# Attention and two MLPs on one core: one tile per PSUM bank in place of tiles of two banks, and another order of the first block

## The chip, the core and the metric

The kernel runs on one core of a Trainium2 chip. A core has a matrix engine (TensorE, PE in the profile), a vector engine (DVE), a scalar engine (ACT), GpSimd (POOL) and SyncE (SP), which here issues all the transfers. Each engine works through its own list of instructions in order; engines wait for each other at semaphores. Matrix results go to PSUM, which has eight banks; a bank holds 512 fp32 values in each of 128 partitions. The metric is the device time of one execution in microseconds, lower is better.

## The reference

The reference is a chunked attention, then an MLP that takes the maximum of three projections, then a second MLP with a piecewise square.

```python
for c in range(nc):                       # 24 chunks of 32 queries; B=4, H=8, S=768, D=64
    k_full = concat([mem_k, k[l_start:r_end]])     # 8 memory keys, 16 left, 32 own, 8 right
    scores = scale * q_c @ k_full.T
    a = exp(scores - max(scores)); a = a / (sum(a) + 1e-9)
    out[c] = a @ v_full
x = out.reshape(3072, 512)
h = maximum(maximum(x @ w1, x @ w2), x @ w3)       # 512 -> 768
x = h @ w_out                                      # 768 -> 512
h = x @ w_in                                       # 512 -> 2048
g = where(h >= 1, h, where(h <= -1, 0, (h + 1)**2 / 4))
out = g @ w_out2                                   # 2048 -> 512
```

## The kernel before

The 3072 tokens are six blocks of 512, and each block is four attention units of 128 tokens (24 units, `u`). Every product of the MLPs is done with operands split into a high and a low part, so one product is three matmuls (`mm3`, L510: high by high, high by low, low by high).

A unit runs: transposes of K and Q (`st_k` L262, `st_q` L293), scores (`st_s`, 32 small matmuls into two banks, one for even heads `e=0` and one for odd heads `e=1`), the row maximum and its subtraction (`st_m` L381, on DVE), exp (`st_e`), row sums and division (`st_n`), the transpose of the weights (`st_a`), the product with V (`st_o`, again two banks), its copy to SBUF (`cp_o` L438), and the transpose and split that give the MLP its input (`st_x`, `cp_x`, `cp_xl` L456).

PSUM is held in tiles of two banks. The scores and the outputs of a unit take a whole such tile (`ps_pair`, L212); the other steps take its two halves in turn (`ps_bank`, L207). In block 0 there are four pairs; from the step `l0` on, one pair is left to attention (L744), two banks (`ps_mm`) belong to the first product of either MLP, and four banks, as two tiles of two (`ps_acc`), hold the sums of the second product.

Those sums are filled slot by slot: `slot_l2` (L551) adds one of the K1 = 6 parts of the first MLP, `slot_l4` (L600) one of the K2 = 16 parts of the second, to the four banks `acc[0..3]`, three matmuls each. In the last slot of a block, each bank is copied out right after its three matmuls: in `slot_l2` by ACT (L565), in `slot_l4` by ACT for `t` 0 and 2 (L617) and by DVE for 1 and 3 (L615).

All engines' lists are written by hand. Block 0 follows the table `PLAN` (L40), a list of step names: `f` loads a raw weight, `wa wh wg ws wp` turn it into the high and low parts (`convert_w`, `hi_w`, `rest_w`, `sub_w`, `add_w`, L125 to L168), `l3` is one product of 12 matmuls, `lt` its maximum, `m0` one `slot_l2`, `d` four small matmuls with nothing but the identity, `lk lq lv lm` loads, and the others the steps of a unit. Further tables say which engine takes a step (`ON_DVE`, `NORM_ON_POOL`, `ABS_ON_ACT` and so on). From block 1 on the order comes from loops (L749): a slot of 12 matmuls, then one step of a later block's attention. In the second MLP the slots alternate, `slot_l4(n)` then `slot_l3(n+3)` (L758).

Of the kernel before, what the change touches and what calls it, by code (L numbers as in the profile page):

```python
# [39 lines left out]
PLAN = """  # L40
lq0 f0 lmem0 wa0 d0 wg0 tq0 lk1 d7 lk0 mem0 f1 wh0 d4 tk1 ws0 ck1 wa1 tk0 wp0 ck0 lq1 f2 lk2 ek0 tq1
ek1 lq2 kw0 cq1 cq0 s0 tk2 lq3 wh1 lk3 ck2 ws1 tq2 tk3 lk4 wg1 wa2 ek2 cq2 mx0 wh2 ex0 d5 wp1 kw1
lm0 tq3 f3 lq4 tk4 wg2 n0 ck3 f4 s1 ek3 a0 kw2 ws2 lk5 ck4 cq3 mx1 lv0 ek4 s2 wp2 wa3 f5 d1 mx2 tq4
tk5 ex1 wg3 wh3 ws3 wa4 kw3 mv0 lv1 ex2 s3 ck5 wp3 n1 wh4 wg4 ca0 lq5 lv2 mv2 cq4 a1 n2 ek5 mv1 o0
co0 ws4 a2 wa5 x0 kw4 ca1 wh5 mx3 f6 o1 tq5 wg5 s4 co1 wp4 ca2 lk6 ex3 ws5 wa6 f7 kw5 lk7 wg6 tk6
lv3 wp5 n3 wa7 mx4 lk8 wh6 o2 ck6 cq5 x1 ws6 wp6 cx0 wh7 cx1 a3 dx0 ex4 f8 wg7 co2 ca3 dx1 n4 ws7
wa8 tk7 ck7 o3 x2 lq6 cx2 s5 f9 co3 wp7 wh8 x3 a4 wg8 mx5 dx2 cx3 dx3 wa9 lv4 tk8 ws8 tq6 ca4 l3 wg9
f10 o4 l0 ex5 wh9 n5 ws9 wp8 wp9 ek7 ek6 wa10 co4 lt3 wg10 wh10 l1 lt0 lt1 l2 f11 wa11 ws10 lv5 lt2
wg11 lm1 cq6 x4 f12 wp10 lh2 wh11 cx4 l4 f13 l5 wa12 wg12 ws11 wp11 lt4 lt5 wh12 a5 dx4 l6 wa13 d6
f14 lk9 wg13 wh13 ws12 ws13 lq7 l7 wp12 lt6 wa14 ca5 lh5 kw6 o5 co5 f15 s6 mx6 wh14 lt7 lv6 wg14 ex6  # L50
l9 wp13 ws14 wp14 lt9 f16 wa15 x5 ck8 n6 tq7 cq7 l10 cx5 wh15 dx5 lt10 wg15 lk10 l8 a6 wa16 ws15 lt8
ek8 ca6 f17 kw7 l11 s7 lt11 wg16 wp15 wa17 m0 l12 wh16 mv6 f18 lm2 mx7 ws16 wg17 wp16 lh8 f19 ex7
wa18 wh17 ws17 m1 wh18 o6 wp17 ws18 l13 co6 d2 wg18 wp18 wa19 lt12 tk9 lq8 wh19 x6 wg19 f20 cx6 ck9
dx6 lt13 m2 n7 f21 lv7 wa20 wh20 wg20 ek9 ws19 wp19 ws20 d3 l14 a7 lt14 tq8 cq8 l15 ca7 wa21 f22
wp20 wa22 o7 lh11 wh21 f23 co7 wh22 lh14 ws22 wg22 l16 kw8 wp22 x7 wg21 ws21 cx7 wp21 m3 lt15 l17
dx7 lt16 s8 lq9 mx8 lk11 wa23 wh23 ws23 wg23 lt17 m4 ex8 wp23 lq10 lv8 lh17
# [12 lines left out]


@with_exitstack
def attention_then_two_mlps(ctx, tc, q, k, v, mem_k, mem_v, w1, w2, w3, w_mid, w_in, w_out, out):
# [132 lines left out]
    pairs, turn = [ps_t.tile([P, 2, TB], F32, name="pt")], [0]

    def ps_bank():  # L207
        i = turn[0] = turn[0] % (2 * len(pairs))
        turn[0] += 1
        return pairs[i // 2][:, i % 2] if not isinstance(pairs[i // 2], list) else pairs[i // 2][i % 2]  # L210

    def ps_pair():  # L212
        i = (turn[0] + 1) // 2 % len(pairs)
        while isinstance(pairs[i], list):
            i = (i + 1) % len(pairs)
        turn[0] = 2 * i + 2
        return pairs[i]

# [629 lines left out]
```

## Time and profile before

| what | value |
|---|---|
| median of 3 runs (lowest to highest) | 1109.12 us (1107.56 to 1109.77) |
| the profiled execution: its time, its span | 1109.17 us, 1107.4 us |
| PE busy | 1038.5 us, 94% of the span |
| weight load (PEld) busy | 833.9 us, 75% |
| DVE busy | 544.8 us, 49% |
| ACT busy | 346.2 us, 31% |
| POOL busy | 243.3 us, 22% |
| mean granted TensorE clock | 0.975 of full |

The span counts from the first to the last instruction of the profiled execution. A row of the trace gives an instruction's start, its duration, engine and source line, what it writes and reads, and in square brackets the idle time of its engine just before and the instruction that ended it. Matmuls overlap in the array: a matmul of 512 columns is shown as 0.39 us long, and the next one starts 0.23 us after it. So the idle time before a matmul is counted from the end of that 0.39, and the distance from one start to the next says more.

### The profile page before, as it was taken

To read this page: it belongs to the slowest core of one execution; us is meant where nothing else is said; L and a number is where in the kernel's file an instruction comes from. 1 tells how busy PE (TensorE), PEld (TensorE's weight loads), DVE (VectorE), ACT (ScalarE), POOL (GpSimd) and SP (SyncE) were. 2 spreads that over 40 slices of the span, in tenths; PEclk is the share of its full clock that TensorE was granted. 3 is DMA by queue.
4 is the path that set the end of the run, shared out by engine and by line. 5 is a ranking of instruction groups with operands and counts; after the bars stand their busy time and mean duration, and the time that the engine had idled before them with its cause. 6 is when DMAs were issued, how large, how long until landed. Compare 5 with 4: busy or idle time off the path is not lost.

```text
span 1107.4 us, 18192 instructions
## 1 busy us (share of the span) xinstructions
PE 1038.5 (94%) x7426; PEld 833.9 (75%) x7426; DVE 544.8 (49%) x896; ACT 346.2 (31%) x609; POOL 243.3 (22%) x193
## 2 busy tenths in 40 slices
PE   6488999999999999999899989989999998998998
PEld 4376768878877778878688868868877886886886
DVE  7999947678777777534454222222222222222221
ACT  4754543342233232243433222212222222222221
POOL 2423221011011011112123213312322321331221
PEclk9689999999999999999899989989999999999999
DMA  9744536556556563243321010010001001001001
GB/s 220 175 130 121 157 80 162 120 139 163 132 139 167 113 171 92 91 133 124 105 66 29 1 49 20 10 47 10 20 1 48 29 1 48 20 1 39 0 1 39
DMA packets 163940, 88.89 MB, mean 80 GB/s; under 512 B 126736, under 2 KB 144144, under 8 KB 163856
## 3 DMA queue, kind: packets, MB, share of 16 engines
q1 hardware_dynamic: 163856, 87.72, 29.6%
q8 instruction: 58, 0.95, 0.4%
q14 instruction: 26, 0.21, 0.1%
HBM read 67.24 MB, written 20.45 MB: 79 GB/s over the span
## 4 chain that ended last, share of the span: by engine, by line
PE 81%; DVE 11%; ACT 3%; issue 2%; SPq 1%; DMA 0%; POOL 0%; ACTq 0%; DVEq 0%; POOLq 0%
PE l L511 15%; PE l L512 15%; PE l L513 15%; PE o L609 8%; PE o L611 8%; PE o L610 8%; PE y L511 3%; PE y L512 2%; PE y L513 2%; PE pt L435 1%; PE pt L371 1%; DVE c_a L136 1%; DVE c_a L138 1%; SPq L345 1%; ACT y L565 1%
## 5 line engine op out<-in xcount | busy, mean ns | idle before, releaser
L596 DVE SCALAR_TENSOR_TENSOR u<-u 128x512 f32<-128x512 f32 x96 | 66.6, 694 | 359.5 <-ACT u L595 359.5
L523 POOL TENSOR_TENSOR hl_b<-u,hh_b 128x512 fp32r<-128x512 f32 x96 | 123.8, 1290 | 409.3 <-ACT hh_b L521 197.9
L511 PE MATMUL l<-xh,hi_a 128*128 128x512 f32 x432 | 175.3, 406 | 4.5 <-DVE xl L458 2.8
L609 PE MATMUL o<-hi_d,hh_b 128*128 128x512 f32 x384 | 152.9, 398 | 17.9 <-ACT ob L617 17.9
L512 PE MATMUL l<-xl,hi_a 128*128 128x512 f32 x432 | 169.4, 392 | 0.0
L513 PE MATMUL l<-xh,lo_a 128*128 128x512 f32 x432 | 169.4, 392 | 0.0
L511 PE MATMUL l<-yh,hi_c 128*128 128x512 f32 x384 | 152.6, 397 | 0.0
L512 PE MATMUL l<-yl,hi_c 128*128 128x512 f32 x384 | 152.4, 397 | 0.0
L513 PE MATMUL l<-yh,lo_c 128*128 128x512 f32 x384 | 152.0, 396 | 0.0
L611 PE MATMUL o<-hi_d,hl_b 128*128 128x512 f32 x384 | 151.4, 394 | 0.0
L610 PE MATMUL o<-lo_d,hh_b 128*128 128x512 f32 x384 | 151.4, 394 | 0.0
L595 ACT ACTIVATE u<-l 128x512 f32<-128x512 f32 x96 | 57.3, 597 | 250.5 <-PE l L513 209.8
L523 POOL TENSOR_TENSOR hl_a<-t,hh_a 128x512 fp32r<-128x512 f32 x33 | 45.0, 1364 | 333.6 <-ACT hh_a L521 333.6
L521 ACT CAST hh_b<-u 128x512 fp32r<-128x512 f32 x96 | 59.6, 620 | 146.2 <-DVE u L597 146.2
L609 PEld LDWEIGHTS o<-hi_d,hh_b 128*128 128x128 f32 x384 | 72.7, 189 | 38.9 <-ACT ob L617 23.6
L511 PEld LDWEIGHTS l<-xh,hi_a 128*128 128x128 f32 x432 | 81.3, 188 | 22.4 <-DVE xl L458 3.0
L513 PEld LDWEIGHTS l<-xh,lo_a 128*128 128x128 f32 x432 | 81.4, 188 | 18.3 <-DVE lo_a L168 0.4
L512 PEld LDWEIGHTS l<-xl,hi_a 128*128 128x128 f32 x432 | 81.6, 189 | 15.2
L511 PEld LDWEIGHTS l<-yh,hi_c 128*128 128x128 f32 x384 | 73.6, 192 | 16.3
L512 PEld LDWEIGHTS l<-yl,hi_c 128*128 128x128 f32 x384 | 73.6, 192 | 16.4
L513 PEld LDWEIGHTS l<-yh,lo_c 128*128 128x128 f32 x384 | 73.5, 191 | 16.4
L611 PEld LDWEIGHTS o<-hi_d,hl_b 128*128 128x128 f32 x384 | 73.0, 190 | 16.0
(167 smaller groups left out, 1334.4 us busy)
## 6 DMA issues: line engine op xcount, KB each, us to landing
st_a<-in_moe_w_dram SPq DMA_DIRECT2D x18, 512.0 KB
vw<-in_v_dram SPq DMA_DIRECT2D x160, 56.0 KB
st_c<-in_moe_w_in_dram SPq DMA_DIRECT2D x16, 512.0 KB
st_d<-in_moe_w_out_dram SPq DMA_DIRECT2D x16, 512.0 KB
yd<-y SPq DMA_DIRECT2D x24, 256.0 KB
yr<-yd SPq DMA_DIRECT2D x24, 256.0 KB
out_dram<-ob SPq DMA_DIRECT2D x24, 256.0 KB
wd<-c_c SPq DMA_DIRECT2D x16, 256.0 KB
```

The lines of the kernel that those rows point to most:

```text
L136: V.tensor_scalar(out=c, in0=c, scalar1=3, scalar2=0x3FFFFFFF, op0=ALU.logical_shift_left, op1=ALU.bitwise_and)
L138: V.scalar_tensor_tensor(out=c, in0=up, scalar=0xC0000000, in1=c, op0=ALU.bitwise_and, op1=ALU.bitwise_or)
L511: nc.tensor.matmul(ps, whi, xhi, start=first, stop=False)
L512: nc.tensor.matmul(ps, whi, xlo, start=False, stop=False)
L513: nc.tensor.matmul(ps, wlo, xhi, start=False, stop=last)
L521: nc.scalar.copy(out=hi, in_=h)
L523: e.tensor_tensor(out=lo, in0=h, in1=hi.bitcast(F32), op=ALU.subtract)
L595: nc.scalar.activation(out=a, in_=ps, func=AF.Relu, bias=0.5, scale=0.5)
L596: nc.vector.scalar_tensor_tensor(out=a, in0=a, scalar=1.0, in1=a, op0=ALU.min, op1=ALU.mult)
L609: nc.tensor.matmul(acc[t], hi[:, c], whi, start=first, stop=False)
L610: nc.tensor.matmul(acc[t], hi[:, c], wlo, start=False, stop=False)
L611: nc.tensor.matmul(acc[t], lo[:, c], whi, start=False, stop=last)
```

## The change

Every PSUM tile becomes one bank. `ps_tile` takes the next pool in the list `psum_turn`: eight turns over the pools `t`, `mm` and `acc0` to `acc3` up to `l0`, after that only the two banks of `ps_t`. The scores and outputs of a unit are two tiles, one for each parity `e`; the maximum and the subtraction (`st_m`) and the copy of the outputs (`cp_o`) become one instruction for each parity, of half the size. The sums of the second products are four tiles with tags of their own, `acc0` to `acc3`. `PLAN` has the same 388 step names in another order, and the tables that choose engines differ.

```diff
-lq0 f0 lmem0 wa0 d0 wg0 tq0 lk1 d7 lk0 mem0 f1 wh0 d4 tk1 ws0 ck1 wa1 tk0 wp0 ck0 lq1 f2 lk2 ek0 tq1
...
+f0 d7 d6 f1 lk0 tk0 lq0 wa0 lm0 lk1 ck0 wa1 lmem0 tq0 wg1 mv0 mv1 lq1 ek0 wh0 lq2 ws0 tk1 ck1 ek1
...
-ca4 co1 cq1 cq4 ek2 ek5 mem0
+ck1 co4 co5 ek0 ek1 ek6 kw0 mem0 mv0
...
-NORM_ON_POOL = "n1 n2 n3 n6 n8".split()
-ABS_ON_ACT = "a1.1 a0.2 a1.2 b.1 a2.2 a0.3 b.2 a0.4 a1.4 b.3 a2.4 a0.5 a1.5 b.4 a2.5 b.5".split()
-LOW_ON_POOL = "a1.0 a2.1 a1.2 a1.3 b.5".split()
-SUB_ON_DVE = "a0.0 a2.0 a1.1 a0.2 a1.2 b.1 a0.3 a1.3 a2.3 a0.4 b.3 a2.4 a1.5 b.4 a2.5".split()
-ADD_ON_DVE = "a1.0 a0.1 b.0 b.1 a0.3 a1.3 a1.4 b.3 a2.4 b.4 a2.5".split()
-SPLIT_ON_DVE = "a0_3 a0_1 a0_2".split()
-SUM_ON_ACT = [5]
+NORM_ON_POOL = "n4 n6".split()
+ABS_ON_ACT = "a0.0 a1.1 b.1 a2.2 a1.3 b.2 a2.3 a0.4 a1.4 a2.4 a0.5 a1.5 b.4 a2.5 b.5".split()
+LOW_ON_POOL = "a1.0 b.0 a1.2 b.2 b.4 b.5".split()
+SUB_ON_DVE = "a1.0 b.1 a0.3 b.2 a2.3 a0.4 b.3 a0.5 a1.5 b.4 a2.5".split()
+ADD_ON_DVE = "a0.0 a1.0 a1.1 a2.1 a0.2 b.1 a1.3 a2.3 b.3 a2.4 a1.5 b.4 a2.5".split()
+SPLIT_ON_DVE = "a0_0 a0_1 a0_2".split()
+SUM_ON_ACT = [7]
...
-    ps_t = ctx.enter_context(tc.tile_pool(name="ps_t", bufs=1, space=PSUM))
+    ps_t = ctx.enter_context(tc.tile_pool(name="ps_t", bufs=2, space=PSUM))
...
+    psum_turn = []
+
+    def ps_tile(name):
+        pool, tag = psum_turn[0]
+        psum_turn.append(psum_turn.pop(0))
+        return pool.tile([P, TB], F32, tag=tag, name=name)
...
-        s = ps_pair()
+        s = [ps_tile(f"s{u}_{e}") for e in range(2)]
...
-        nc.vector.tensor_reduce(out=m, in_=sg, axis=AX.X, op=ALU.max)
+        for e in range(2):
+            nc.vector.tensor_reduce(out=m[:, e], in_=sg[e], axis=AX.X, op=ALU.max)
...
-            nc.vector.tensor_tensor(
-                out=p.rearrange("p h e j -> p e h j"), in0=sg, in1=m.to_broadcast([P, 2, HP, NK]), op=ALU.subtract)
+            for e in range(2):
+                nc.vector.tensor_tensor(
+                    out=p[:, :, e], in0=sg[e], in1=m[:, e].to_broadcast([P, HP, NK]), op=ALU.subtract)
...
-        copy("co", u)(out=xs[u].rearrange("p (h e d) -> p e h d", h=HP, e=2), in_=pp.pop(("o", u)))
+        for e, o in enumerate(pp.pop(("o", u))):
+            copy("co", u)(
+                out=xs[u].rearrange("p (h e d) -> p e h d", h=HP, e=2)[:, e],
+                in_=o[:, 0:HP * D].rearrange("p (h d) -> p h d", h=HP))
...
-            if f == 0 and d % 2 == 0:
-                t = ps_acc.tile([P, 2, TB], F32, tag="acc", name=f"y{j}_{d}", bufs=2)
-                acc[d], acc[d + 1] = t[:, 0], t[:, 1]
+            if f == 0:
+                acc[d] = ps_acc.tile([P, TB], F32, tag=f"acc{d}", name=f"y{j}_{d}")
...
-            if first and t % 2 == 0:
-                o2 = ps_acc.tile([P, 2, DM], F32, tag="acc", name=f"o{i}_{t}", bufs=2)
-                acc[t], acc[t + 1] = o2[:, 0], o2[:, 1]
+            if first:
+                acc[t] = ps_acc.tile([P, DM], F32, tag=f"acc{t}", name=f"o{i}_{t}")
...
+        psum_turn += [(ps_t, "t"), (ps_mm, "mm"), (ps_acc, "acc0"), (ps_acc, "acc1"),
+                      (ps_t, "t"), (ps_mm, "mm"), (ps_acc, "acc2"), (ps_acc, "acc3")]
```

Three places show what this does to the engines' lists. The first is on PE, the last `slot_l4` of a block (here the last block; `o_0` and `o_2` are the two tiles of two banks, `hh` and `hl` the split input, and a bracket names the engine whose semaphore the row waits for). Before:

```order
L609 MATMUL o_0_8900<-hi_d_6240,hh_b_15_9327 128x512 [waits Activation_49]
L610 MATMUL o_0_8900<-lo_d_6241,hh_b_15_9327 128x512
L611 MATMUL o_0_8900<-hi_d_6240,hl_b_15_9328 128x512 [waits Pool_49]
L609 MATMUL o_0_8900<-hi_d_6240,hh_b_15_9327 128x512 [waits Activation_49]
L610 MATMUL o_0_8900<-lo_d_6241,hh_b_15_9327 128x512
L611 MATMUL o_0_8900<-hi_d_6240,hl_b_15_9328 128x512
L609 MATMUL o_2_8907<-hi_d_6240,hh_b_15_9327 128x512
L610 MATMUL o_2_8907<-lo_d_6241,hh_b_15_9327 128x512
L611 MATMUL o_2_8907<-hi_d_6240,hl_b_15_9328 128x512
L609 MATMUL o_2_8907<-hi_d_6240,hh_b_15_9327 128x512 [waits Activation_49]
```

Now, with a tile for each bank:

```order
L603 MATMUL o_0_9166<-hi_d_6498,hh_b_15_9595 128x512 [waits Activation_49]
L604 MATMUL o_0_9166<-lo_d_6499,hh_b_15_9595 128x512
L605 MATMUL o_0_9166<-hi_d_6498,hl_b_15_9596 128x512 [waits Pool_49]
L603 MATMUL o_1_9170<-hi_d_6498,hh_b_15_9595 128x512
L604 MATMUL o_1_9170<-lo_d_6499,hh_b_15_9595 128x512
L605 MATMUL o_1_9170<-hi_d_6498,hl_b_15_9596 128x512
L603 MATMUL o_2_9174<-hi_d_6498,hh_b_15_9595 128x512
L604 MATMUL o_2_9174<-lo_d_6499,hh_b_15_9595 128x512
L605 MATMUL o_2_9174<-hi_d_6498,hl_b_15_9596 128x512
L603 MATMUL o_3_9178<-hi_d_6498,hh_b_15_9595 128x512
```

The waits for ACT and POOL in the first product, which are for the split input, stay; those ahead of the second and the fourth bank are no longer there. The second place is on DVE, early in block 0, the maximum and subtraction of unit 0 and what follows them (`c_a`, `st_a` are a raw weight's stages, `m` and `p` maximum and weights of a unit). Before:

```order
L384 TENSOR_REDUCE m_251<-pt 128x8
L389 TENSOR_TENSOR p_253<-pt,m_251 128x2x4x64
L168 TENSOR_TENSOR lo_a_0_226<-c_a_0_160,st_a_0_145 128x512
L151 TENSOR_SCALAR st_a_0_172<-c_a_0_243 128x512
L157 SCALAR_TENSOR_TENSOR st_a_0_172<-st_a_0_172 128x512
L411 TENSOR_REDUCE r_281<-p_253 128x8
```

Now:

```order
L377 TENSOR_REDUCE m_256<-s_0_186 128x4
L377 TENSOR_REDUCE m_256<-s_1_187 128x4
L383 TENSOR_TENSOR p_259<-s_0_186,m_256 128x4x64
L383 TENSOR_TENSOR p_259<-s_1_187,m_256 128x4x64
L168 TENSOR_TENSOR lo_a_0_223<-c_a_0_135,st_a_0_116 128x512
L134 TENSOR_SCALAR c_a_1_268<-st_a_1_253 128x512
L135 TENSOR_SCALAR c_a_1_268<-c_a_1_268 128x512
```

Two instructions became four of half the size, and another weight's conversion stands behind them. The third place is the start of SP's list, the first transfers (`st_a` a raw weight of 512 KB, `kq` Q or K of a unit, 256 KB). Before:

```order
L232 DMA kq<-in_q_dram 128x8x64
L117 DMA st_a_0_110<-in_moe_w_dram 128x4x256
L692 DMA memk<-in_mem_k_dram 128x2x64 x2
L226 DMA kq<-in_k_dram 128x8x64 x2
L117 DMA st_a_0_145<-in_moe_w_dram 128x4x256
```

Now:

```order
L117 DMA st_a_0_104<-in_moe_w_dram 128x4x256
L117 DMA st_a_0_116<-in_moe_w_dram 128x4x256
L218 DMA kq<-in_k_dram 128x8x64
L224 DMA kq<-in_q_dram 128x8x64
L232 DMA mv_130<-in_mem_v_dram 8x4x64 x2
L218 DMA kq<-in_k_dram 128x8x64
L686 DMA memk<-in_mem_k_dram 128x2x64 x2
```

Two weights now stand ahead of the first K and Q.

## Rows read from the trace of the kernel before

**Rows 1.** The span in five stretches: busy time of each engine (and its instructions), granted clock of PE, busy share of the DMA engines, GB/s.

```profile
0.00:65.00 65.00, 36.09 (x763) 28.02 (x764) 56.08 (x110) 39.06 (x69) 20.77 (x23) 0.82 0.80 192
65.00:87.00 22.00, 20.30 (x146) 16.14 (x146) 19.83 (x33) 9.87 (x28) 7.00 (x5) 0.92 0.34 94
87.00:148.00 61.00, 58.14 (x632) 45.70 (x632) 57.81 (x98) 28.81 (x52) 13.80 (x10) 1.00 0.54 140
148.00:555.00 407.00, 393.30 (x3618) 313.10 (x3617) 259.95 (x442) 134.07 (x235) 54.99 (x41) 0.99 0.49 130
555.00:1107.00 552.00, 530.65 (x2273) 430.98 (x2271) 151.10 (x216) 134.44 (x226) 146.77 (x114) 0.98 0.07 23
```

**Rows 2.** All waits of PE from 148 us to the end: for what, microseconds in total, times, the longest.

```profile
PE o L609 <- ACT ob L617: 17.9, 12, 2.6
PE y L511 <- ACT y L565: 12.0, 12, 4.6
PE pt L421 <- DVE p L415: 0.9, 1, 0.9
PE pt L435 <- ACT aT L425: 0.7, 1, 0.7
```

**Rows 3.** Instructions in order of time around the end of the second block of the second MLP.

```profile
726.95 0.40 PE L609 MATMUL o<-hi_d,hh_b 128*128 128x512 f32 x1
...
732.49 0.40 PE L609 MATMUL o<-hi_d,hh_b 128*128 128x512 f32 x1
...
732.96 0.39 PE L611 MATMUL o<-hi_d,hl_b 128*128 128x512 f32 x1
...
734.83 0.62 ACT L521 CAST hh_b<-u 128x512 fp32r<-128x512 f32 x1 [1.48 <-DVE u L597]
735.36 0.58 ACT L617 COPY ob<-o 128x512 f32<-128x512 f32 x1
...
735.99 0.80 PE L609 MATMUL o<-hi_d,hh_b 128*128 128x512 f32 x1 [2.64 <-ACT ob L617]
...
739.59 0.79 PE L609 MATMUL o<-hi_d,hh_b 128*128 128x512 f32 x1 [0.68 <-ACT ob L617]
...
745.87 0.39 PE L609 MATMUL o<-hi_d,hh_b 128*128 128x512 f32 x1
```

**Rows 4.** PE at the end of block 1 of the first MLP, where two matmuls start 0.23 us apart unless they wait.

```profile
240.79 0.40 PE L513 MATMUL y<-hh_a,lo_b 128*128 128x512 f32 x1
241.86 0.50 PE L511 MATMUL y<-hh_a,hi_b 128*128 128x512 f32 x1 [0.68 <-ACT y L565]
242.20 0.40 PE L512 MATMUL y<-hl_a,hi_b 128*128 128x512 f32 x1
```

**Rows 5.** The same at the end of the first MLP's last block.

```profile
542.17 0.39 PE L513 MATMUL y<-hh_a,lo_b 128*128 128x512 f32 x1
547.18 0.50 PE L511 MATMUL y<-hh_a,hi_b 128*128 128x512 f32 x1 [4.62 <-ACT y L565]
```

**Rows 6.** Stretches around ends of blocks, columns as in rows 1; the first is the first MLP's last block, the others are blocks of the second MLP.

```profile
546.00:556.00 10.00, 8.15 (x22) 5.99 (x23) 2.09 (x2) 3.40 (x7) 1.27 (x1) 0.66 0.48 161
642.00:651.00 9.00, 8.33 (x25) 6.26 (x24) 1.38 (x2) 1.07 (x2) 0.47 (x1) 0.62 0.43 147
735.00:746.00 11.00, 9.34 (x22) 6.89 (x23) 1.38 (x2) 1.52 (x3) 1.26 (x1) 0.53 0.34 119
828.00:838.00 10.00, 6.68 (x28) 4.79 (x27) 2.77 (x4) 2.49 (x5) 1.28 (x1) 1.00 0.35 121
922.00:928.00 6.00, 4.06 (x11) 2.78 (x12) 0.85 (x3) 1.69 (x3) 1.27 (x1) 0.72 0.29 107
1013.00:1023.00 10.00, 6.68 (x28) 4.81 (x27) 2.77 (x4) 2.84 (x5) 1.27 (x1) 1.00 0.29 106
```

**Rows 7.** Groups of instructions of DVE, first from 0 to 148 us, the last two from the whole span: line, engine, operation, tiles, shapes, count, busy us and mean ns of one, idle before.

```profile
L134 DVE TENSOR_SCALAR c_a<-st_a 128x512 uint32<-128x512 uint32 x7 | 4.1, 591 | 4.5 <-DMA st_a<-in_moe_w_dram 4.5
L157 DVE SCALAR_TENSOR_TENSOR st_b<-st_b 128x512 f32<-128x512 uint32 x5 | 3.5, 694 | 0.2
L384 DVE TENSOR_REDUCE m<-pt 128x8 f32<-128x512 f32 x7 | 4.8, 682 | 0.4 <-PE pt L371 0.4
L348 DVE STREAM_TRANSPOSE kw<-kq 128x512 f32<-128x512 f32 x12 | 8.5, 704 | 1.6 <-DMA kq<-in_k_dram 1.6
L356 DVE STREAM_TRANSPOSE qTb<-qs 128x256 f32<-128x256 f32 x12 | 4.4, 408 | 0.0
```

**Rows 8.** Groups of instructions of ACT, columns as in rows 7.

```profile
L291 ACT COPY kw<-kT 128x896 f32<-128x896 f32 x12 | 11.2, 936 | 1.2 <-PE pt L371 1.2
L247 ACT COPY vw<-mv 8x1024 f32<-8x1024 f32 x8 | 8.3, 1044 | 0.1
```

**Rows 9.** Single instructions of block 0, and the first matmul of block 1 (the last row).

```profile
0.74 0.43 SPq L232 DMA_DIRECT2D kq<-in_q_dram  x1
1.22 0.57 SPq L117 DMA_DIRECT2D st_a<-in_moe_w_dram  x1
...
5.93 0.43 DVE L134 TENSOR_SCALAR c_a<-st_a 128x512 uint32<-128x512 uint32 x1 [4.45 <-DMA st_a<-in_moe_w_dram]
...
64.80 0.50 PE L511 MATMUL l<-xh,hi_a 128*128 128x512 f32 x1 [2.75 <-DVE xl L458]
...
147.88 0.39 PE L511 MATMUL l<-xh,hi_a 128*128 128x512 f32 x1
```

More of the change, by code (lines that the diff above doesn't have):

```diff
@@ L40 @@
 PLAN = """
-lq0 f0 lmem0 wa0 d0 wg0 tq0 lk1 d7 lk0 mem0 f1 wh0 d4 tk1 ws0 ck1 wa1 tk0 wp0 ck0 lq1 f2 lk2 ek0 tq1
[L42 to L50, printed above, removed]
@@ new lines @@
+mem0 cq0 wg0 f2 kw0 s0 wh1 wp0 tq2 lk2 lk3 tk2 wa2 tq1 mv2 wh2 f3 ws1 mx0 lq3 cq1 ck2 ek2 wp1 wa3
+tk3 ex0 kw1 ck3 cq2 lk5 lk4 s1 n0 ek3 wg2 tk4 ws2 f4 lq4 kw2 s2 tq3 wg3 mx1 wp2 ck4 wh3 cq3 ex1 ek4
+a0 lv0 d0 mx2 ca0 ex2 n1 wa4 tq4 kw3 f5 a1 o0 ws3 ca1 wh4 wp3 tk5 ck5 wg4 ek5 s3 wa5 co0 kw4 ws4 n2
+cq4 lk6 f6 x0 a2 lv1 wh5 wp4 lv2 wg5 ws5 lk7 wa6 o1 cx0 s4 co1 wh6 wg6 mx3 dx0 lq5 tk6 ca2 tq5 ck6
+wp5 ws6 mx4 f7 ex3 ex4 tk7 d1 n3 wp6 kw5 lv3 cq5 a3 ck7 o2 ca3 f8 wa7 x1 co2 n4 o3 x2 s5 cx2 lq6 cx1
@@ new lines @@
+lk8 ek7 wg7 wh7 ws7 a4 wa8 wg8 dx1 tq6 ek6 mx5 lv4 d3 co3 x3 ca4 dx2 f9 wh8 wp7 tk8 lq7 f10 cx3 dx3
+o4 l3 co4 ex5 ws8 wa9 lt3 cq6 wg9 d4 x4 wp8 tq7 wh9 l0 n5 ws9 kw6 wa10 a5 wp9 wg10 ck8 lt0 d5 ca5
+f11 wh10 wa11 wg11 lk9 ws10 ek8 wp10 lv5 l1 o5 l2 co5 lt1 wh11 lm1 s6 l4 lt2 ws11 mx6 mv6 f12 wa12
+wp11 kw7 lh2 f13 cq7 cx4 lq9 lt4 dx4 x5 wh12 l6 wa13 lq8 d2 m0 ws12 cx5 l5 wh13 f14 wg13 wg12 wp12
+dx5 ws13 wp13 ex6 wa14 lt6 lm2 f15 n6 wg14 lt5 wh14 l9 wa15 lh5 ws14 a6 ca6 f16 wp14 l10 wg15 s7 m1
@@ L57 @@
+lt9 wh15 ws15 f17 wa16 wh16 l7 lv6 mx7 lt10 ex7 l8 wg16 wp15 lk10 ws16 wa17 wh17 wp16 wg17 f18 lt7
+o6 f19 lt8 co6 tk9 ws17 x6 ck9 l11 wp17 wa18 tq8 wh18 wg18 lt11 lh8 wa19 cx6 ws18 dx6 f20 lh11 wp18
+l12 n7 wh19 m2 ek9 lq10 lt12 ws19 wg19 lv7 wa20 cq8 wp19 l13 lt13 a7 f21 ca7 l14 o7 wg20 wa21 wh20
+ws20 co7 l15 wh21 wg21 wp20 x7 f22 ws21 lt14 wa22 f23 lk11 kw8 cx7 wg22 wh22 m3 dx7 l16 lt15 lh14
+ws22 wp22 wp21 lt16 wa23 wg23 wh23 ws23 s8 l17 lt17 lh17 mx8 lv8 m4 ex8 wp23
 """.split()
 ON_DVE = """
-ca4 co1 cq1 cq4 ek2 ek5 mem0
+ck1 co4 co5 ek0 ek1 ek6 kw0 mem0 mv0
@@ L203, in attention_then_two_mlps @@
     xh, xl = {}, {}
[L205 to L217, printed above, removed]
+    psum_turn = []
[3 more added lines that the diff above has]
+        return pool.tile([P, TB], F32, tag=tag, name=name)
     def copy(kind, u):
@@ L364, in st_s @@
         ub = u % UPB
-        s = ps_pair()
-        pp["s", u] = sg = s[:, :, 0:HP * NK].rearrange("p e (h j) -> p e h j", h=HP)
+        s = [ps_tile(f"s{u}_{e}") for e in range(2)]
+        pp["s", u] = sg = [t[:, 0:HP * NK].rearrange("p (h j) -> p h j", h=HP) for t in s]
         for h in range(HP):
@@ L427, in st_o @@
     def st_o(u):
-        o = ps_pair()
-        pp["o", u] = o[:, :, 0:HP * D].rearrange("p e (h d) -> p e h d", h=HP)
+        pp["o", u] = o = [ps_tile(f"o{u}_{e}") for e in range(2)]
         a = aT.pop(u)
@@ L435, in st_o @@
                     nc.tensor.matmul(
-                        o[t, e, h * D:(h + 1) * D], a[r, h, t], vws[u][r, c, h], start=True, stop=True)
+                        o[e][t, h * D:(h + 1) * D], a[r, h, t], vws[u][r, c, h], start=True, stop=True)
     def cp_o(u):
         xs[u] = at.tile([P, DM], F32, tag="xs", name=f"xs{u}")
-        copy("co", u)(out=xs[u].rearrange("p (h e d) -> p e h d", h=HP, e=2), in_=pp.pop(("o", u)))
+        for e, o in enumerate(pp.pop(("o", u))):
+            copy("co", u)(
+                out=xs[u].rearrange("p (h e d) -> p e h d", h=HP, e=2)[:, e],
+                in_=o[:, 0:HP * D].rearrange("p (h d) -> p h d", h=HP))
     def st_x(u):
         x = xs.pop(u)
-        pp["x", u] = t = ps_bank().rearrange("p (h t) -> p h t", h=KD)
+        pp["x", u] = t = ps_tile(f"tx{u}").rearrange("p (h t) -> p h t", h=KD)
         for h in range(KD):
@@ L704, in attention_then_two_mlps @@
         nc.vector.memset(vw[64:96, 0], 0.0)
-        pairs.append([ps_mm.tile([P, TB], F32, tag="mm", name=f"pm{i}") for i in range(2)])
-        pairs.extend(ps_acc.tile([P, 2, TB], F32, tag="acc", name=f"pa{i}", bufs=2) for i in range(2))
+        psum_turn += [(ps_t, "t"), (ps_mm, "mm"), (ps_acc, "acc0"), (ps_acc, "acc1"),
+                      (ps_t, "t"), (ps_mm, "mm"), (ps_acc, "acc2"), (ps_acc, "acc3")]
         def mem_t(_):
-            tm = ps_bank()[:, 0:B // 2 * P].rearrange("p (o b h m) -> p o b h m", o=B // 2, b=2, h=H)
+            tm = ps_tile("tm")[:, 0:B // 2 * P].rearrange("p (o b h m) -> p o b h m", o=B // 2, b=2, h=H)
             for o in range(B // 2):
@@ L743, in attention_then_two_mlps @@
             if name == "l0":
-                del pairs[1:]
+                del psum_turn[:]
+                psum_turn += [(ps_t, "t")]
             run(kind, i)
```

22 lines of the change are left out of this document (8 added, 14 removed).

## The prediction

> **What bounds the kernel now.** I read the busy time by stretches first, then PE's waits, then single instructions where a wait sits, and last the groups of block 0. The stretches [rows 1] show two regimes. Up to 148 us, block 0, DVE is busy 56.08 + 19.83 + 57.81 = 133.7 us and PE 36.09 + 20.30 + 58.14 = 114.5 us of 148. PE's idle 33.5 us lie nearly all before its first large product at 64.80 [rows 9]; from 65 us to 148 us PE idles 4.6 us and DVE 5.4 us, so there both are full. After 148 us PE is busy all but 13.7 us up to 555 us and all but 21.4 us after it, while DVE has 147 us free in the first of these and 401 us in the second. PE is the bound there, and what it loses is a wait. The list of waits [rows 2] has two large rows: 17.9 us in 12 waits of the second product of the second MLP for ACT's copy of a finished bank, 12.0 us in 12 waits of the same kind in the first MLP. Both are the last slot of a block: PE has finished the first bank of a two-bank tile, ACT copies it, and the matmul that writes the other bank stands until the copy is done. A larger attention wait than 0.9 us is not there.
>
> **The waits at the ends of blocks, the first term.** With a tile for each bank the second and the fourth bank no longer wait for the copy of their neighbour; PE's list shows it. That takes away 24 waits and 29.9 us of shown idle. Each costs more than the idle shown: in [rows 4] the starts 240.79 and 241.86 are 1.07 us apart where 0.23 is usual, so the wait with 0.68 of idle costs 0.84, and the next start comes 0.34 later instead of 0.23. That is 0.16 + 0.11 = 0.27 for each wait, and 24 of them make 6.5 us. [Rows 5] agrees: 5.01 - 0.23 = 4.78 for an idle of 4.62. First term: 29.9 + 6.5 = 36.4 us.
>
> **The clock behind them, the second term.** In [rows 3] two slots take 732.49 - 726.95 = 5.54 us when nothing is wrong, and 745.87 - 732.49 = 13.38 us at the end of the block: 7.84 us lost. The two waits there explain 2.64 + 0.68 + 2 x 0.27 = 3.86 us. The other 3.98 us are matmuls at the lower clock: [rows 6] has 0.53 for the 11 us from 735, that is 2 x 0.47 x 11 = 10.3 us at 1.2 instead of 2.4 GHz, and the drop follows an idle of 2.64 us on PE. So a microsecond at the lower clock costs 3.98 / 10.3 = 0.39 us. The other stretches give 2 x 0.34 x 10 = 6.8, 2 x 0.38 x 9 = 6.8 and 2 x 0.28 x 6 = 3.4 us of it, and those at 828 and 1013 none: 27.3 us in all, 10.5 us lost. If the idle goes, I expect PE to keep the full clock, as it does around the other ends. If it does not, this term is nothing; if it goes in full, it is the 10.5 I take.
>
> What is late next at these places. At 732.49 the last slot would run to 735.2, the next slot of the other product to 738.0, and only then is the first bank written again. ACT is free for the first copy at 735.36, behind its cast at 734.83 [rows 3], and takes 0.58 for each copy, so the banks are free 1.5 us or more ahead. At 542.17 it is tighter [rows 5]: ACT's first copy ends at about 547.1, and with one slot between (2.75 us) PE would come back to the first bank at about 547.2. The other banks follow at 0.69 for three matmuls against 0.58 for a copy. I count nothing lost there; it could be 1 us.
>
> **The split instructions.** Scores and outputs of a unit are read by two instructions of half the size. The trace has no half-size maximum or subtraction. The nearest rows are the transposes on DVE, 704 ns for 512 elements and 408 ns for 256 [rows 7]: two halves cost 0.11 us more than the whole. From below it is nothing (a time that goes with size alone); from above a half costs as much as a whole, 0.68 us as the maxima of L384 do [rows 7]. I take 0.11, from the only pair that differs in size alone. In blocks 1 to 5 (15 units) this is 2 x 0.11 on DVE and some 0.2 on ACT for a unit, hidden in DVE's 147 us and ACT's 273 us of free time up to 555 us; without that cover it would be 15 x 0.42 = 6.3 us. In block 0 there are nine maxima and eight subtractions: 17 x 0.11 = 1.9 us on DVE, between 0 and 11.6.
> The Trainium skill's page "VectorE: DVE Perf Modes" (section on the TRN2 errata) speaks against the change: a DVE instruction with an SBUF source has a measured fixed part of about 150 cycles, and it advises tiles of 512 elements or more. As an estimate at 0.96 GHz that is 0.16 us for each extra instruction, and the sum for block 0 would be 2.7 instead of 1.9 us. The rows agree that a fixed part is there, with 0.11, and none shows it for a PSUM source.
>
> **Block 0, the third term.** DVE sets its pace, so I count what the tables put on DVE and take off, each 512-element instruction 0.69 us as on L157 [rows 7]. One more mask on DVE instead of ACT: +0.43 (the first in [rows 9]). One product more on POOL: -0.69. Subtractions on POOL 13 instead of 9: -2.76. Additions on DVE two more: +1.38. Divisions on DVE two more: +1.38. Together -0.3. Copies: four of 0.69 and two edge fills of about 0.34 go (3.4); in come `ck1` 0.69, one edge fill 0.34 (units 0 and 6 have none), four output halves of 0.41, `kw0` and the two of `mv0`. Those three were on ACT, at 0.94 and 2 x 1.04 [rows 8]. For DVE, 0.43 to 0.69 for 512 elements bounds them at 2.5 to 4.0; I take ACT's 3.0. That makes +2.2. With the halves: -0.3 + 2.2 + 1.9 = +3.8 us of DVE work.
> At the start the first weight is issued first. SP issued it 0.48 us after Q [rows 9], and 256 KB of Q at 192 GB/s [rows 1] are 1.4 us: DVE can begin up to 1.9 us earlier than 5.93, at worst at the same time. The first K and Q come behind 1 MB of weights, so the first scores come later by some microseconds; DVE has two weights to convert meanwhile, and if that cover fails, 3 us are lost. How well the new order fills the gaps can't be read from the rows: between -4.6 - 1.9 = -6.5 (every wait of PE after 65 us gone and the early start kept, with the added work in the gaps of DVE) and 3.8 + 3 + the 2 of a pessimistic half = +9. I take 3.8 - 1.9 = +1.9.
>
> **Sum.** 36.4 + 10.5 = 46.9 us saved after 148 us, 1.9 us lost before. The profiled execution took 1109.17 us, 1.8 us more than its span of 1107.4 and 0.05 from the median of 1109.12, so nothing is to be corrected: 1109.2 - 46.9 + 1.9 = 1064 us.
>
> **The rivals.**
> - DVE makes block 0 longer. For it: DVE is busy 90% of block 0 and gets 3.8 us more. A half from PSUM may cost well over the transposes' rate: at 0.35 more than I count for each of the 17, it is 6 us. 1064 + 8 = 1072 us.
> - The new order fills PE's gaps. For it: 33.5 us of idle and a clock of 0.82 up to 65 us [rows 1] are there to be won, and halves of a pair no longer wait for each other in block 0 either. Against it: DVE has no room before 65 us (56.08 of 65). With the first large product 6 us earlier and the 4.6 us of later waits gone, less what the sum has: about 1054 us.
> - Only the idle goes, the clock still drops. For it: the ends at 828 and 1013 had the same 2.64 us of idle without a drop, so idle alone does not decide. 1064 + 10.5 = 1074.5 us.
> - Slower than before: attention in blocks 1 to 5 stalls PE on its two banks. A unit's scores take both, and each needs two readers to let go. If every one of the six steps of a unit that write PSUM waited 0.9 us, as the one in [rows 2] did, 15 units would lose 81 us and the time would be 1145; from 3.1 us for a unit it is slower than before. Against it: the same two banks serve now with 1.6 us of such waits in all.
> - It doesn't do what it says: the waits stay in another form, for instance on the copies before the next block's first slot, 1109 us. Against it: there are 2.75 us of other matmuls before those.
>
> **How the numbers follow.** Forecast 0.60, with its own range of 1058 to 1070; DVE longer 0.17; gaps filled 0.15; clock still low 0.04; attention stalls 0.03; no effect 0.01. The range 1053 to 1075 takes in the first four but for their tails. What differs by less than 0.2% (2 us) can't be told from no change here. The first four cases are all faster: 0.96. No effect 0.01, slower 0.03.
>
> **What would show it.** Right: no row of PE waiting for the copies of `y` and `o` among the waits; a granted clock of 1.00 in each stretch after block 0; the first matmul of block 1 near 150 us; the last block of the second MLP and all others of the same length. Wrong: PE waiting at the first slot of a block's sums, a clock below 1 after 200 us, the first matmul of block 1 later than 157 us or earlier than 141, or PE waits for ACT or DVE at the small matmuls of scores and outputs of some microseconds in sum.

## The result

The changed kernel takes 1071.1 us, the median of 4 runs (1070.44 to 1072.04), the kernel before 1109.44 on the same chip (1107.56 to 1111.35): a ratio of 0.9655, 95% interval 0.9637 to 0.9673, 38.3 us faster. The forecast was 1064 with a range of 1053 to 1075. The profiled execution took 1070.82 us, with a span of 1069.0.

The stretches of the changed kernel, cut and laid out as in [rows 1]:

```profile
0.00:65.00 65.00, 35.72 (x750) 27.61 (x750) 53.32 (x115) 35.50 (x69) 19.18 (x21) 0.89 0.76 178
65.00:87.00 22.00, 20.95 (x278) 16.53 (x279) 20.14 (x40) 11.46 (x22) 6.85 (x5) 0.92 0.69 185
87.00:148.00 61.00, 56.24 (x491) 44.25 (x491) 59.32 (x98) 28.48 (x66) 18.05 (x13) 0.97 0.44 123
148.00:555.00 407.00, 402.99 (x3678) 324.93 (x3677) 267.43 (x486) 137.97 (x257) 55.10 (x41) 1.00 0.50 133
555.00:1069.00 514.00, 510.25 (x2234) 419.22 (x2232) 146.88 (x212) 131.16 (x221) 145.56 (x113) 1.00 0.07 23
```

After 148 us PE now idles 4.0 us up to 555 us (13.7 before) and 3.8 us after it (21.4 before), and the granted clock is 1.00 in both stretches. Up to 148 us PE is busy 112.9 us against 114.5 and DVE 53.32 + 20.14 + 59.32 = 132.8 against 133.7, but block 0 isn't over at 148 us any more, as the end of this section shows.

All waits of PE from 148 us to the end, the counterpart of [rows 2]:

```profile
PE ta L415 <- DVE p L409: 2.6, 1, 2.6
PE o L428 <- ACT aT L419: 0.7, 1, 0.7
PE l L507 <- DVE t L535: 0.7, 1, 0.7
PE l L509 <- DVE lo_a L168: 0.4, 1, 0.4
```

The 24 waits for the copies of `y` and `o`, 29.9 us, are gone. The small row for the attention weights `p`, 0.9 us before, has grown to 2.6, and a wait for `t` has come up beside it.

The end of a block of the first MLP, in order of time, as [rows 4] shows it for another block (PE's rows first, then ACT's of the same time):

```profile
321.81 0.39 PE L507 MATMUL y<-hh_a,hi_b 128*128 128x512 f32 x1
322.04 0.40 PE L508 MATMUL y<-hl_a,hi_b 128*128 128x512 f32 x1
322.27 0.39 PE L509 MATMUL y<-hh_a,lo_b 128*128 128x512 f32 x1
322.50 0.40 PE L507 MATMUL y<-hh_a,hi_b 128*128 128x512 f32 x1
...
321.31 2.67 ACT L560 COPY y<-y 128x512 f32<-128x512 f32 x4
```

ACT copies four banks from 321.31 to 323.98, and PE writes the next of them meanwhile at its usual 0.23 us from start to start; where [rows 4] have 1.07 between two starts, nothing is left. Writing one bank while another is read costs PE nothing here; what stopped it before was that both banks belonged to one tile. The Trainium skill's page "PSUM — Partial Sum Buffer" (section "Summary: rules for kernel authors") tells to aim matmuls at a different bank while one is read and to guard by bank. The kernel before followed the first half, and the guard was wider than a bank; the trace puts the price of that at 29.9 us of idle and what follows it.

The first matmul of block 1, the last of [rows 9], and the first large product before it:

```profile
69.19 0.50 PE L507 MATMUL l<-xh,hi_a 128*128 128x512 f32 x1
...
152.73 0.39 PE L507 MATMUL l<-xh,hi_a 128*128 128x512 f32 x1
```

Block 0 ends 152.73 - 147.88 = 4.85 us later than before. So the span splits in two: 4.85 us lost up to block 1, and from there 959.5 us (1107.4 - 147.88) have become 916.3 (1069.0 - 152.73), 43.2 us saved. The first large product alone is already 4.39 us late.

### The profile page after: what moved, and what is told of

The parts are those of the page before. It is cut to its first block, busy times and chain, and to the rows that moved or that the text cites. A ratio compares the mean times of both kernels' runs of the same rounds, so it can differ in the third digit from the quotient of the medians.

```text
span 1069.0 us, 18282 instructions
## 1 busy us (share of the span) xinstructions
PE 1026.2 (96%) x7426; PEld 832.5 (78%) x7426; DVE 547.1 (51%) x946; ACT 344.6 (32%) x631; POOL 244.7 (23%) x193
## 4 chain that ended last, share of the span: by engine, by line
PE 84%; DVE 11%; DMA 2%; issue 1%; ACT 1%; SPq 1%; POOL 0%; DVEq 0%; ACTq 0%
PE l L507 16%; PE l L509 16%; PE l L508 16%; PE o L605 8%; PE o L603 8%; PE o L604 8%; PE y L507 3%; PE y L508 3%; PE y L509 3%; PE o L428 1%; PE s L363 1%; DVE c_a L136 1%; DVE c_a L138 1%; DVE st_a L157 1%; PE tx L442 1%
## 5 line engine op out<-in xcount | busy, mean ns | idle before, releaser
L603 PE MATMUL o<-hi_d,hh_b 128*128 128x512 f32 x384 | 149.9, 390 | 0.0
```

What stands on the lines that cost most here:

```text
L603: nc.tensor.matmul(acc[t], hi[:, c], whi, start=first, stop=False)
```

## The experiments

All kernels were profiled, and timed beside the kernel before on their own chip. There the kernel before took 1107.04 us (sums in pairs, weight ahead, layout only) and 1105.36 us (the other four), and the ratios go by these. For each, the table splits the profiled span at the first matmul of block 1, as above.

| kernel | block 1 begins | from there to the end | median (lowest to highest), runs | ratio to before, 95% |
|---|---|---|---|---|
| before | 147.88 | 959.5 | 1109.44 (1107.56 to 1111.35), 4 | |
| changed | 152.73 | 916.3 | 1071.1 (1070.44 to 1072.04), 4 | 0.9655 (0.9637 to 0.9673) |
| changed, a second time | 152.91 | 915.4 | 1069.61 (1068.20 to 1070.53), 6 | 0.9661 (0.9630 to 0.9692) |
| sums in pairs | 152.78 | 957.3 | 1110.65 (1105.94 to 1114.08), 10 | 1.0036 (1.0015 to 1.0058) |
| weight ahead | 153.12 | 910.7 | 1065.26 (1064.81 to 1065.59), 6 | 0.9624 (0.9593 to 0.9654) |
| layout only | 164.18 | 916.5 | 1081.13 (1079.34 to 1085.61), 6 | 0.9773 (0.9742 to 0.9803) |
| old turn, old order | 147.51 | 915.9 | 1063.57 (1062.29 to 1065.23), 5 | 0.9610 (0.9578 to 0.9641) |
| halves only | 149.11 | 954.7 | 1107.82 (1102.17 to 1113.09), 12 | 1.0015 (0.9990 to 1.0040) |
| old turn, weight ahead | 147.15 | 910.4 | 1059.44 (1059.26 to 1060.74), 5 | 0.9574 (0.9544 to 0.9605) |

The two columns of times move independently of each other, and each experiment moves mainly one of them: the sums and the weight decide the second, the turn of banks and the order the first.

**Sums in pairs.** The changed kernel, with the sums of the second products back in tiles of two banks; everything else stays.

```diff
-    ps_acc = ctx.enter_context(tc.tile_pool(name="ps_acc", bufs=1, space=PSUM))
+    first = ExitStack()
+    ps_acc = first.enter_context(tc.tile_pool(name="ps_acc", bufs=1, space=PSUM))
...
-            if f == 0:
-                acc[d] = ps_acc.tile([P, TB], F32, tag=f"acc{d}", name=f"y{j}_{d}")
+            if f == 0 and d % 2 == 0:
+                t = late["acc"].tile([P, 2, TB], F32, tag="acc", name=f"y{j}_{d}", bufs=2)
+                acc[d], acc[d + 1] = t[:, 0], t[:, 1]
...
+            if name == "m0":
+                first.close()
+                late["acc"] = ctx.enter_context(tc.tile_pool(name="ps_acc2", bufs=2, space=PSUM))
```

Expected: 

> The changed kernel with the sums of the second products back in tiles of two banks from the first one on; all else stays. Theory (the ends of blocks gave 46.9 us): the 24 waits are back with 28 to 31 us of idle, clock dips follow them, and the time is 1108 to 1118 us. Rival (most of the gain came from the order of block 0 or from attention's single banks): under 1095 us.

Measured: 1110.65 us. PE's waits from 155 us to the end:

```profile
PE o L607 <- ACT ob L615: 17.9, 12, 2.6
PE y L509 <- ACT y L563: 12.0, 12, 4.6
PE o L430 <- ACT aT L421: 0.7, 1, 0.7
PE ta L417 <- DVE p L411: 0.5, 1, 0.5
```

The two rows are back with the counts and sums of [rows 2], and 957.3 - 916.3 = 41 us with them. So the whole gain of the change comes from the tiles of the sums; without them it gains nothing, and the ratio of 1.0036 is a loss of about the size of block 0's. The wait for `p` is small again: PE, stopped at the ends of blocks, comes later to it.

**Weight ahead.** In the changed kernel I looked for what is late now. DVE, in order of time, around the wait for `p`:

```profile
351.08 0.43 DVE L135 TENSOR_SCALAR c_c<-c_c 128x512 f32<-128x512 f32 x1 [4.95 <-ACT c_c L132]
...
352.62 0.68 DVE L535 TENSOR_TENSOR t<-l,t 128x512 f32<-128x512 f32 x1
...
353.52 0.76 DVE L377 TENSOR_REDUCE m<-s 128x4 f32<-128x256 f32 x2
...
358.15 0.69 DVE L409 TENSOR_TENSOR p<-p,r 128x512 f32<-128x512 f32 x1
```

DVE stands 4.95 us for a raw weight on its way through ACT, and everything behind it in its list is late: `t`, then the attention steps up to `p`. PE and ACT at the same place, and SP's list, which issued that weight:

```profile
350.39 0.66 ACT L132 ACTIVATE c_c<-st_c 128x512 f32<-128x512 f32 x1 [6.60 <-DMA st_c<-in_moe_w_in_dram]
...
353.36 0.50 PE L507 MATMUL l<-xh,hi_a 128*128 128x512 f32 x1 [0.65 <-DVE t L535]
...
358.99 1.02 PE L415 MATMUL ta<-ident,p 128*128 128x128 f32 x4 [2.62 <-DVE p L409]
...
360.24 0.63 PE L508 MATMUL l<-xl,hi_a 128*128 128x512 f32 x1
360.66 0.63 PE L509 MATMUL l<-xh,lo_a 128*128 128x512 f32 x1
...
337.36 7.98 SPq L337 DMA_DIRECT2D qs<-in_q_dram  x15
...
345.88 0.43 SPq L117 DMA_DIRECT2D st_c<-in_moe_w_in_dram  x1
```

SP spends 7.98 us on issuing 15 small transfers of Q, 0.53 us each, and the weight's transfer stands behind them, issued at 345.88. After the wait PE's matmuls start 0.42 us apart (360.24, 360.66) instead of 0.23. The stretch around it, columns as in [rows 1], with the granted clock of 0.87:

```profile
352.00:365.00 13.00, 9.72 (x97) 7.25 (x96) 11.54 (x25) 2.81 (x6) 1.66 (x1) 0.87 0.58 148
```

The edit lets that step ask for the weight before the attention steps of the slot put their transfers into SP's list:

```diff
+                part = (s + 1 + (s > 1)) % 6
+                ahead = part == 2
+                if ahead:
+                    round_step(BY_PART[part], 3)
                 for _ in range(2 if s == 2 else 1):
                     att_step()
...
-                part = (s + 1 + (s > 1)) % 6
                 feed((4, 5, 3, 5, 4, 0)[part])
-                round_step(BY_PART[part], 3)
+                if not ahead:
+                    round_step(BY_PART[part], 3)
```

Expected: 

> The changed kernel, where in one of six slots of blocks 1 to 4 the next raw weight is asked for before the pending loads of Q and K are flushed, not after them. Theory (the 5.0 us lost at 352 to 363 us come from a raw weight that stood behind 16 small transfers: ACT waited 6.6 us for it, DVE for ACT, the maximum and the division of a unit behind that, PE for these): ACT's wait for the raw weight shrinks below 2 us, PE's wait of 2.6 us goes, the clock stays at 1.00 there, and the time is 1065 to 1068 us. Rival (PE is simply ahead of attention there since it no longer stops at the ends of blocks): a wait of 2 us or more stays and the time is 1070 to 1073 us.

Measured: 1065.26 us. SP's list, then DVE's first instruction on that weight:

```profile
335.40 0.43 SPq L117 DMA_DIRECT2D st_c<-in_moe_w_in_dram  x1
335.93 8.71 SPq L337 DMA_DIRECT2D qs<-in_q_dram  x15
...
344.96 0.43 DVE L135 TENSOR_SCALAR c_c<-c_c 128x512 f32<-128x512 f32 x1
```

The weight is asked for 10.5 us earlier, and DVE waits no more. Of PE's waits from 155 us on a single one is left, 0.7 us, and around the old place PE is busy throughout, at the full clock:

```profile
340.00:365.00 25.00, 25.00 (x253) 20.11 (x236) 18.81 (x37) 9.11 (x17) 2.50 (x2) 1.00 0.57 127
```

From block 1 on it takes 916.3 - 910.7 = 5.6 us less (4.7 against the second execution of the changed kernel): that is what the stall costs, two waits of 3.3 us in all and a stretch of lower clock behind them.

The weight was late in the kernel before too. DVE's first instruction on it there, and PE's wait for `p`:

```profile
349.11 0.43 DVE L135 TENSOR_SCALAR c_c<-c_c 128x512 f32<-128x512 f32 x1 [3.40 <-ACT c_c L132]
...
357.23 0.63 PE L421 MATMUL pt<-ident,p 128*128 128x128 f32 x4 [0.92 <-DVE p L415]
```

DVE stood 3.40 us there, and little of it reached PE. SP issued that weight at 343.97; counted from the first matmul of block 1, it now issues it 2.9 us earlier (345.88 - 152.73 = 193.15 against 196.09). But PE, which no longer stops at the ends of blocks, now stands ready for `p` 4.8 us earlier (358.99 - 2.62 - 152.73 = 203.64 against 357.23 - 0.92 - 147.88 = 208.43), and so a lateness that was nearly covered shows.

**Layout only.** The changed kernel with `PLAN` and the tables of engines of the kernel before.

```diff
-f0 d7 d6 f1 lk0 tk0 lq0 wa0 lm0 lk1 ck0 wa1 lmem0 tq0 wg1 mv0 mv1 lq1 ek0 wh0 lq2 ws0 tk1 ck1 ek1
...
+lq0 f0 lmem0 wa0 d0 wg0 tq0 lk1 d7 lk0 mem0 f1 wh0 d4 tk1 ws0 ck1 wa1 tk0 wp0 ck0 lq1 f2 lk2 ek0 tq1
...
-SUM_ON_ACT = [7]
+SUM_ON_ACT = [5]
```

Expected: 

> The changed kernel with the table of block 0 and the engine tables of before; the one-bank tiles and the halved instructions stay. Theory (the new order and its tables cost block 0 its 4.9 us, the first matmul of block 1 came at 152.7 instead of 147.9 us): block 1 begins between 146 and 150 us and the time is 1064 to 1067 us. Rival (the halved instructions and the turn of single banks cost it, whatever the order): block 1 begins at 152 us or later and the time stays at 1070 to 1073 us. In both no wait for the copies of y and o.

Measured: 1081.13 us, block 1 begins at 164.18. The time lies above both ranges. My theory, that the new order itself costs block 0 its microseconds, falls: with the order of before the loss is 16.3 us instead of 4.85. PE's waits up to 165 us:

```profile
PE l L507 <- DVE t L535: 8.5, 5, 4.2
PE o L428 <- DVE xl L454: 7.9, 1, 7.9
PE ta L415 <- POOL p L409: 6.1, 2, 4.5
```

The second row is the telling one. The outputs `o` are made from `aT` and V alone; `xl` is a step that reads another tile, `tx`. PE waits 7.9 us for it because `o` gets the bank that `tx` was in. So my next theory was that the order of before fits the turn in which banks were handed out then, and waits under the new one; the new order gets 11.5 of the 16.3 us back. Of the changed kernel's own waits up to 148 us at least three are of the same kind, 11.3 us in all: the transposes of K waiting for the subtraction that reads the scores, a step with nothing but the identity (`warm`) waiting for `xl`, and transposes of K again, waiting for the copy of the outputs. How much of this costs time can't be read from it, since DVE and not PE sets the pace of block 0:

```profile
PE tk L258 <- DMA kq<-in_k_dram: 5.1, 2, 4.2
PE ta L415 <- DVE p L409: 4.9, 3, 2.4
PE tk L258 <- DVE p L383: 4.8, 1, 4.8
PE warm L718 <- DVE xl L454: 4.4, 1, 4.4
...
PE tk L258 <- ACT xs L434: 2.1, 1, 2.1
```

**Old turn, old order.** If that is so, the one-bank tiles must do no harm where they are handed out as before: scores and outputs take an aligned pair of banks, the other steps the next bank. `PLAN` and the tables are those of before, as in "layout only".

```diff
+    def ps_two(names):
+        i = (turn[0] + 1) // 2 * 2 % len(psum_turn)
+        while psum_turn[i][1] == "mm":
+            i = (i + 2) % len(psum_turn)
+        turn[0] = i
+        return [ps_tile(n) for n in names]
...
-        s = [ps_tile(f"s{u}_{e}") for e in range(2)]
+        s = ps_two([f"s{u}_{e}" for e in range(2)])
...
-        psum_turn += [(ps_t, "t"), (ps_mm, "mm"), (ps_acc, "acc0"), (ps_acc, "acc1"),
-                      (ps_t, "t"), (ps_mm, "mm"), (ps_acc, "acc2"), (ps_acc, "acc3")]
+        psum_turn += [(ps_t, "t0"), (ps_t, "t1"), (ps_mm, "mm"), (ps_mm, "mm"),
+                      (ps_acc, "acc0"), (ps_acc, "acc1"), (ps_acc, "acc2"), (ps_acc, "acc3")]
```

Expected: 

> One-bank tiles and halved instructions as in the changed kernel, but the banks are taken in the turn of before (scores and outputs take the two banks of an aligned pair, single tiles the next bank) and block 0 follows the order and engine tables of before. With the new turn the old order let block 1 begin at 164.2 us instead of 147.9. Theory (the turn of the banks does not fit the old order: a tile waits for the reader of the bank that is next, though others are free): block 1 begins at 148 to 151 us, the stall near 352 us stays, and the time is 1066 to 1070 us. Rival (the halved instructions cost the old order its 16 us, as DVE paces block 0): block 1 begins at 160 us or later and the time stays at 1078 to 1083 us.

Measured: 1063.57 us, 2.4 us below the range. Block 1 begins at 147.51, where it was before the change (147.88), the waits for the sums are gone, and the stall of DVE behind the weight is still there. With "layout only" beside it, same order and same tables, the turn of the banks alone moves the start of block 1 by 16.7 us. It shows as idle time of DVE: up to block 1 DVE is busy 133.11 us of 164.18 there and 135.13 of 147.51 here, so it idles 31.1 and 12.4 us. The new order with the old turn wasn't tried, so how the 4.85 us would divide between turn and order stays open.

**Halves only.** The kernel before, with the maximum, the subtraction and the copy of the outputs as two halves each, in its own tiles of two banks.

```diff
-        nc.vector.tensor_reduce(out=m, in_=sg, axis=AX.X, op=ALU.max)
+        for e in range(2):
+            nc.vector.tensor_reduce(out=m[:, e], in_=sg[:, e], axis=AX.X, op=ALU.max)
...
+            for e in range(2):
+                nc.vector.tensor_tensor(
+                    out=p[:, :, e], in0=sg[:, e], in1=m[:, e].to_broadcast([P, HP, NK]), op=ALU.subtract)
...
+        for e in range(2):
+            copy("co", u)(out=xs[u].rearrange("p (h e d) -> p e h d", h=HP, e=2)[:, e], in_=o[:, e])
```

Expected: 

> The kernel before, with the maximum, the subtraction and the copy of the outputs issued as two instructions of half the size; tiles of two banks, order and tables stay. Theory (a pair of halves takes 0.07 to 0.15 us longer than the whole on DVE, and only block 0 feels it): 1108 to 1112 us, block 1 begins at 148.5 to 151 us. Rival (the halves cost the old order in block 0 its 16 us): block 1 begins at 160 us or later, 1120 to 1127 us.

Measured: 1107.82 us, a ratio of 1.0015 (0.9990 to 1.0040): nothing that the time can tell (and 0.2 us below the range expected). In the profile block 1 begins at 149.11, 1.2 us later than before. That the halves also cost nothing visible under "old turn, old order" fits a term that is partly covered.

**The changed kernel again**, on the chip of the last two, as a measure of what one profile is worth.

Expected: 

> The changed kernel once more, on the chip of the other three, as what they are compared with: 1069 to 1073 us, block 1 begins at 152 to 153.5 us.

Measured: 1069.61 us; block 1 begins at 152.91 instead of 152.73, so the start of block 1 can be read to some tenths.

**Old turn, weight ahead.** The kernel of "old turn, old order" with the edit of "weight ahead".

Expected: 

> The first kernel of this group (turn, order and tables of before, one-bank tiles) with the raw weight asked for ahead of the pending loads. Theory (the two costs are independent, 4 us in block 0 and 5 us near 352 us): 1060 to 1064 us, faster than the changed kernel with the weight ahead alone (1065.3 us). Rival (the old order brings its own stalls or block 0 does not recover): 1066 us or more.

Measured: 1059.44 us, 0.6 below the range, 0.9574 of before (0.9544 to 0.9605), 4.1 us below "old turn, old order" and 10.2 us below the changed kernel, both on the same chip (1063.57 and 1069.61). The two edits add up: 147.15 to block 1, and 910.4 from there. It is the best of the kernels here.

## Why the prediction came out as it did

The time lay 7 us above the forecast, inside its range, and the direction and size were those of its first two terms.

**Waits and clock at the ends of blocks, 46.9 us: right.** All 24 waits went and the clock is 1.00 in the long stretches. From block 1 on 43.2 us are saved; with the new stall taken away, 959.5 - 910.7 = 48.8. The counter-test, in which the stall is nearly hidden again, is 41.0 us longer than the changed kernel and 957.3 - 910.7 = 46.6 longer than the one without the stall, from one execution whose clock fell at other ends. The 10.5 us for the clock is a figure of one execution (see the last section). Taking it in full was right, since without these waits the clock stays at 1.00 at the ends of blocks; that the sum is met within 2 us is in part luck, since 17 executions of the kernel before on one chip lie between 1102.0 and 1112.36 us. The step that I called tight, the last block of the first MLP, cost next to nothing, as the counterpart of [rows 5] shows:

```profile
546.09 1.55 ACT L560 COPY y<-y 128x512 f32<-128x512 f32 x3
...
546.77 0.45 PE L603 MATMUL o<-hi_d,hh_b 128*128 128x512 f32 x1
547.06 0.39 PE L604 MATMUL o<-lo_d,hh_b 128*128 128x512 f32 x1
```

ACT's first copy starts at 546.09, PE writes that bank at 546.77, and the next start is 0.06 us later than the usual 0.23.

**"What is late next at these places": the step that failed.** It looked only at the ends of blocks and at the banks there. The place that became late is elsewhere, and [rows 2] had its row: 0.9 us for `p`. I read it as evidence that attention waits little, when it was a wait that PE's own stops had kept small, while DVE stood 3.40 us at the weight. "Sums in pairs" shows it: with the stops back that wait is 0.5. The price is 5 us, from 4.7 to 5.6.

**Block 0, 1.9 us lost: right in sign, too small; 4.85.** Up to the first matmul of block 1, first in the kernel before and then in the changed one:

```profile
0.00:147.88 147.88, 114.41 (x1539) 89.74 (x1539) 133.60 (x239) 77.73 (x148) 41.57 (x38) 0.91 0.63 156
0.00:152.73 152.73, 117.64 (x1538) 92.28 (x1539) 137.34 (x260) 77.55 (x158) 45.93 (x41) 0.93 0.60 151
```

DVE is busy 3.74 us more, where the sum counted +3.8; 1.1 us of this are two instructions that came behind that point before (a maximum `t` and a step of a weight). DVE idles 15.39 us instead of 14.28, so 1.11 more, where the sum had 1.9 less. Two terms were wrong there. The early start gave 0.83 instead of 1.9. The rest, 1.11 + 0.83 = 1.94 us, is idle time of DVE inside the block (in the second execution of the changed kernel, busy 138.34 us of 152.91 with DVE's start at 5.07, it is 1.15 and the busy time 4.74), which the step "Block 0, the third term" put at nothing in its sum and left to the range: it counted durations and didn't look at the turn in which banks are handed out, though that is part of the diff. A bank taken in another turn makes a matmul wait for a reader that it has nothing else to do with (`o` for `xl`), and no sum of durations shows that; under the old order it was worth 16.7 us. How much of the 1.2 to 1.9 us comes from the turn and how much from the order isn't shown.

The early start was sized at 1.9 us from the transfers; DVE begins at 5.10 instead of 5.93, so 0.83:

```profile
4.42 0.66 ACT L132 ACTIVATE c_a<-st_a 128x512 f32<-128x512 f32 x1 [2.40 <-DMA st_a<-in_moe_w_dram]
...
5.10 0.43 DVE L135 TENSOR_SCALAR c_a<-c_a 128x512 f32<-128x512 f32 x1 [3.62 <-ACT c_a L132]
```

It waits for ACT now, which takes the first absolute value. ACT starts on the weight at 4.42, 1.51 us before DVE did, and its 0.66 us stand between the transfer and DVE: moving a step to another engine put a second instruction there.

**The halves, 1.9 us in block 0: somewhat high, about 1 us.** The groups of DVE up to 160 us, against the maximum of [rows 7]:

```profile
L377 DVE TENSOR_REDUCE m<-s 128x4 f32<-128x256 f32 x18 | 6.7, 414 | 0.0
L383 DVE TENSOR_TENSOR p<-s,m 128x256 f32<-128x256 f32 x16 | 6.0, 413 | 0.0
```

A half takes 0.414 us where 0.408 was counted, so two of them are 0.15 longer than a whole of 0.68. But a pair back to back, as at 353.52 above, is shown 0.76 long in all: the second begins before the first has ended, and the extra is some 0.07. Seventeen pairs at that price are 1.2 us; the busy column gives 1.0 (6.7 + 6.0 against 9 x 0.682 + 8 x 0.692, the wholes of before), and in "halves only" block 1 begins 1.2 us later. The Trainium skill's page "VectorE: DVE Perf Modes" (section on the TRN2 errata), whose fixed part of about 150 cycles the prediction weighed for an SBUF source, has in its table 120 cycles for a PSUM source, as an estimate 0.125 us at 0.96 GHz. The trace is near that for halves one by one, with 0.15, and not for a pair in a row, with 0.07.

**The three DVE copies, 3.0 us: too high.** `kw0` took 0.62 for 896 elements and the two of `mv0` 0.68 each for 1024, 2.0 in all, below even the lower bound of 2.5, which went by 0.43 us for 512 elements. In the second execution the two of `mv0` took 2.2 together, so that it was 2.8.

**The rivals.** "DVE makes block 0 longer" named nearly the right time, 1072, by luck: its extra 6 us were to come from the halves, and these cost about 1 us, while DVE's work grew by what the sum already had. "Only the idle goes" fell, since the clock is 1.00. "Attention stalls PE on its two banks" fell: of the waits after block 0 the largest, 2.6 us, is for the data `p` and not for a bank, and the others are 0.7 us or less. "The new order fills PE's gaps" fell: up to 65 us PE is busy 35.72 us against 36.09, and the first large product is later.

## What to carry to other kernels

Where PE waits for the copy of a result beside the one it writes, give each PSUM bank a tile of its own before anything else: here that one edit was worth over 40 us, and the rest of the change cost 5. But handing banks out in another turn is an edit of its own that an order written by hand can depend on (16.7 us with the old order); keep the turn, or expect to search the order again. And when a large stop of the bounding engine goes, read every small wait that is left as one that may grow, also at other places, and ask what stands ahead of its transfer in the issuing queue.
